# A chunked scan that feeds a feed-forward layer: two batches, not two heads, stacked in the partitions, tiles of 64 rows in TensorE, and the first feed-forward step one chunk sooner

## The chip, the cores and the metric

One core of a Trainium2 chip runs the whole program. The metric is the device time of one execution in microseconds (us), and the median of the runs is what counts. The profiled execution is one run by itself, with its own time and, beside it, the span from its first to its last instruction.

## The reference, cut to what matters

```python
# x [4, 8, 768, 32], a [4, 8, 768], B and C [4, 8, 768, 16]
for c in range(nc):
    cum = np.cumsum(log_a[chunk c])                       # per batch and head
    L = np.exp(cum[i] - cum[j]) * (i >= j)
    M = einsum('bhin,bhjn->bhij', Cc, Bc) * L
    y[chunk c] = M @ xc + einsum('bhin,bhnd->bhid', Cc, state) * np.exp(cum)
    state = exp(sum(la)) * state + sum_j (Bc[j] xc[j]) * exp(cum[-1] - cum[j])
x = y as [3072 tokens, 256]
h = x @ w_in                                              # 256 -> 2048
out = np.maximum(0.01 * h, h) @ w_out                     # 2048 -> 256
```

A state-space scan goes over 768 steps in chunks, for 4 batches and 8 heads. Its output, 3072 tokens of 256 numbers, goes through a two-layer network (FFN). The FFN's weights come as 64-bit floats, which the kernel turns into two 32-bit parts (a high part `wha` and a rest `wla`), so that each product of the FFN is a sum of three TensorE products.

## The kernel before

**Stages.** The scan takes 12 chunks (`NC`) of 64 tokens (`Q`). Within its loop run the first FFN steps, which need only the first 512 tokens, and the decoding of the first nine weight blocks (128 of the 2048 inner columns each). Behind the scan a middle phase goes through what is left of token blocks 0 and 1 (512 tokens each), and a late phase through blocks 2 to 5. The order of the instructions on each engine is the order of the code: nothing reorders it. DMAs go through SP's queue.

**One chunk c of the scan** (loop `for c in range(2, NC + 1)`), in the order in which TensorE (PE) gets its work:

- `decays`: exponents of the decay factors by one product each for two halves, into `pd` and, in the early chunks, the bank of the FFN's `h`. ScalarE (ACT) takes the exponential into `lt` (`decay_exp`).
- `scores(c)`: C times B, into the banks of `pa` and `pb` (two banks each). `bbd` is B spread by ACT (`spread_b`), so that one product gives both heads of a pair, which lie stacked in the partitions.
- `states(c-1)`: what chunk c-1 adds to the state, into a corner of `pb`.
- `passed(c+1)`: cumulated exponents, four products into another corner of `pb`. ACT takes their exponential `es` (`passed_exp`), GpSimd (POOL) multiplies it with C into `cd` (`weigh_c`).
- `weigh(c, 0)`, `weigh(c, 1)`: VectorE (DVE) multiplies the scores in `pa`, then those in `pb`, with `lt`. `keep_state(c-1)`, two operations on DVE, makes the new state `ss`.
- `ffn_in`: from chunk `FIRST` on, six products of 512 columns into `h`. ACT takes the leaky ReLU twice, DVE the rest.
- `outputs(c-1)`: a part from the state (`cd` times `ss`, the "inter" products) and a part from the chunk itself (`lt` times `x`, the "intra" products), both into `yspace`: bank pair `o01` for the first chunks, columns of `pa` later. `keep_out` copies the sum out on ACT. Two chunks (each 4 batches x 64 tokens) make one token block of 512; for chunks 0 to 3, which fill blocks 0 and 1, the copy goes to `xh`, and `low_out` on DVE takes the rest `xl`. The FFN reads these two as its high and low parts.
- `ffn_out`: six products of 512 columns into `o01`, once two steps are in the queue.

The decoding of a weight block (`dec_abs`, `dec_clamp`, `dec_shift`, `dec_sign`, `dec_low`, `dec_high`, `dec_rest`) is spread over the chunks by the table `duty`: in part -1 it stands ahead of `passed`, in part 0 ahead of `outputs`, in part 1 at the chunk's end.

**PSUM.** The scan holds seven banks besides `h`'s: `o01` (two), `pa` (two), `pb` (two) and `pd`. From chunk `FIRST - 1` on `o01` is left to the FFN's accumulation.

**The middle phase** has one step for (f, block 1) with f below `NEARLY`, and two steps for each later f; a step is six products into `h` and six into `o`.

Of the kernel before, what the change touches and what calls it, by code (L numbers as in the profile page):

```python
# [31 lines left out]
ROW = 64  # L32
PR = ROW + 6
KD = PR + 3 * GB
DIRECT = 1
SLOTS = 5
WARM = 6
FIRST = 5
# [9 lines left out]
def scan_ffn(ctx: ExitStack, tc: tile.TileContext, a_l, bcn_l, x_l, w_l, out_l):  # L48
# [142 lines left out]
    zspace = pb[:, 0, CT:CT + NB * D]  # L191
    espace = pb[:, 1, CT:]
# [22 lines left out]
    erev = cst.tile([128, NC * GB, 2], F32, name="erev")  # L215
# [8 lines left out]
    bs, cs, ts, xs, bbd, bnd, lts, es, cds, ss, tmps = ({} for _ in range(11))  # L224
# [83 lines left out]
    )  # L308
    dve.tensor_reduce(
# [76 lines left out]
    def spread_b(c):  # L386
        bbd[c] = pw.tile([128, NB, 2, Q], F32, name="bbd")
        for hp in range(2):
            act.activation(
                bbd[c][:, :, hp], bs[c].rearrange("p (b i) -> p b i", b=NB), AF.Copy,  # L390
                scale=odd[:, hp:hp + 1],
            )

    def scores(c):
        for b in range(NB):
            for g in range(NG):
                r = slice(32 * g, 32 * g + 32)
                o = b * Q
                pe.matmul(  # L399
                    (pa, pb)[g // 2][:, g % 2, o:o + Q], lhsT=bbd[c][r, b].rearrange("p h i -> p (h i)"),  # L400
                    rhs=cs[c][r, b * Q:(b + 1) * Q], start=True, stop=True,
                )

    def weigh(c, half):
        m = lts[c][:, halves[half]].rearrange("p (g b) i -> p g (b i)", g=2)
        dve.tensor_tensor(out=m, in0=(pa, pb)[half][:, :, :CT], in1=m, op=ALU.mult)

    def states(c):
        for b in range(NB):
            for g in range(NG):  # L410
                gb = g * NB + b
                pe.matmul(  # L412
                    zspace[32 * g:32 * g + 32, b * D:(b + 1) * D],
                    lhsT=bnd[c][:, gb].rearrange("p h n -> p (h n)"), rhs=xs[c][:, gb],
                    start=True, stop=True, skip_group_check=True,
                )

    def keep_state(c):
        ss[c] = p3.tile([128, NB, 2, D], F32, name="ss")
        z = zspace.rearrange("p (b d) -> p b d", b=NB)  # L420
        for hp in range(2):
            if c:
                dve.scalar_tensor_tensor(
                    out=ss[c][:, :, hp], in0=z, scalar=odd[:, hp:hp + 1], in1=tmps[c][:, :, hp],
                    op0=ALU.mult, op1=ALU.add,
                )
            else:
                dve.tensor_scalar(
                    out=ss[c][:, :, hp], in0=z, scalar1=odd[:, hp:hp + 1], scalar2=None,
                    op0=ALU.mult,  # L430
                )

    def end_decay(c):
        tmps[c] = pw.tile([128, NB, 2, D], F32, name="tmp")
        e = es[c].rearrange("p (b i) -> p b i", b=NB)[:, :, Q - 1:]
        pool.tensor_tensor(
            out=tmps[c].rearrange("p b h d -> p b (h d)"),
            in0=ss[c - 1].rearrange("p b h d -> p b (h d)"),
            in1=e.to_broadcast([128, NB, 2 * D]), op=ALU.mult,
        )  # L440

    def weigh_b(c):
        bnd[c] = pw.tile([128, GB, 2, N], F32, name="bnd")
        pool.tensor_tensor(
            out=bnd[c],
            in0=ts[c].rearrange("p (g n) -> p g n", n=N).unsqueeze(2).to_broadcast(
                [128, GB, 2, N]),
            in1=erev[:, c * GB:(c + 1) * GB].unsqueeze(3).to_broadcast([128, GB, 2, N]),
            op=ALU.mult,
        )  # L450
# [7 lines left out]
    def passed(c):  # L458
        for g in range(NG):
            pe.matmul(  # L460
                espace[32 * g:32 * g + 32],
                lhsT=dl[ROW:PR, c].rearrange("p h i -> p (h i)")[:, ::2 * Q // 32],
                rhs=dr[ROW:PR, slot(c), g * NB:(g + 1) * NB].rearrange("p g i -> p (g i)"),
                start=True, stop=True, skip_group_check=True,
            )

    def passed_exp(c):
        es[c] = p3.tile([128, CT], F32, name="es")
        act.activation(es[c], espace, AF.Exp)
# [5 lines left out]
    def outputs(c):  # L475
        mt, y = lts[c], yspace(c)
        if c:
            for b in range(NB):
                for g in range(NG):
                    r = slice(32 * g, 32 * g + 32)  # L480
                    o = 64 * (g % 2)
                    pe.matmul(  # L482
                        y[o:o + 64, g // 2, b * Q:(b + 1) * Q],
                        lhsT=ss[c - 1][r, b].rearrange("p h d -> p (h d)"),
                        rhs=cds[c][r, b * Q:(b + 1) * Q], start=(b == 0), stop=False,
                        skip_group_check=True,
                    )
        for b in range(NB):
            for h in range(NH):
                g, hp = divmod(h, 2)  # L490
                r = slice(64 * hp, 64 * hp + 64)
                o = 32 * (h % 4)
                gb = g * NB + b
                pe.matmul(  # L494
                    y[o:o + 32, h // 4, b * Q:(b + 1) * Q], lhsT=xs[c][r, gb], rhs=mt[r, gb],
                    start=(c == 0 and b == 0), stop=True, skip_group_check=True,
                )

    def keep_out(c):
        t, o = divmod(c, 2)  # L500
        cols = slice(o * CT, (o + 1) * CT)
        act.copy((xh if t < 2 else xf)[t][:, :, cols], yspace(c))

    def low_out(c):
        t, o = divmod(c, 2)
        cols = slice(o * CT, (o + 1) * CT)
        if t < 2:
            dve.tensor_tensor(
                out=xl[t][:, :, cols], in0=yspace(c), in1=xh[t][:, :, cols], op=ALU.subtract,
            )  # L510
# [19 lines left out]
    pool.memset(erev, 0.0)  # L530
# [7 lines left out]
    spread_b(0)  # L538
# [9 lines left out]
    sum_rows(1, o01[:, 0, 2 * Q:4 * Q])  # L548
# [16 lines left out]
    keep_state(0)  # L565
    passed(1)
# [10 lines left out]
    scores(1)  # L577
# [21 lines left out]
    send_rows(4, 6)  # L599
    for c in range(2, NC + 1):  # L600
# [32 lines left out]
        fetch_w(c - 2, (0,) if c > 2 else ())  # L633
# [265 lines left out]
```

## Time and profile before

| | |
|---|---|
| median of 3 runs | 322.34 us (321.31 to 322.8) |
| profiled execution | 321.72 us |
| its span, first to last instruction | 320.0 us |
| mean granted clock of TensorE | 0.993 |
| instructions | 7414 |

The profiled execution is 0.62 us below the median. Its span leaves 1.72 us of it that no instruction covers. An entry such as "32*64 32x64" is a product on a part of the array of 32 rows and 64 columns, with an operand of 32 partitions and 64 elements.

### The profile page before, as it was taken

The page shows a single profiled execution, that of the slowest core. Times are in us where ns is not written, and L with a number is a line of the kernel's source. Part 1 is how long each engine was busy: PE and PEld are TensorE (multiplying, and loading weights), DVE is VectorE, ACT ScalarE, POOL GpSimd, SP SyncE. Part 2 cuts the span into 40 slices and gives each one's busy share as a digit, 9 for nine tenths or more (in the row PEclk, how much of TensorE's full clock was granted, in tenths as well). Part 3 has the DMA queues.
Part 4 walks back from the last instruction along what each step waited for, and adds up shares of the span by engine and source line. Part 5 has one row for each costly group of instructions (what it writes and reads, how often), then busy time and mean ns, then how long its engine had stood idle before and what let it go on. Part 6 is the DMA issues. An engine that isn't in the chain of part 4 may idle for free.

```text
span 320.0 us, 7414 instructions
## 1 busy us (share of the span) xinstructions
PE 309.0 (97%) x3049; PEld 246.7 (77%) x3049; DVE 215.3 (67%) x351; ACT 189.6 (59%) x347; POOL 82.8 (26%) x103
## 2 busy tenths in 40 slices
PE   8799699999999999999999999999999999999994
PEld 3477577777788888888788888888888888888883
DVE  6558787777788999744766666775576555665551
ACT  7668667775569567643765456654475435554351
POOL 4457655662273656820000101000000000000000
PEclk9979999999999999999999999999999999999999
DMA  6759565533324100000210000000012000000003
GB/s 188 217 152 288 170 195 183 175 101 88 115 65 133 67 1 0 2 0 0 81 52 0 0 0 3 1 0 2 0 38 95 0 0 0 2 1 0 0 2 132
DMA packets 15296, 20.40 MB, mean 64 GB/s; under 512 B 3166, under 2 KB 8094, under 8 KB 15262
## 3 DMA queue, kind: packets, MB, share of 16 engines
q1 hardware_dynamic: 14910, 19.84, 19.6%
q8 instruction: 24, 0.39, 0.5%
q10 hardware_dynamic: 352, 0.09, 0.1%
q14 instruction: 10, 0.08, 0.1%
HBM read 16.62 MB, written 3.29 MB: 62 GB/s over the span
## 4 chain that ended last, share of the span: by engine, by line
PE 93%; DVE 2%; ACT 1%; DMA 1%; issue 1%; ACTq 0%
PE o L150 40%; PE h L150 37%; PE pa L399 3%; PE pa L494 3%; PE pa L482 2%; PE pd L453 1%; PE pb L412 1%; PE o L494 1%; DMA dl<-sums 1%; PE pa L246 1%; PE o L482 1%; PE pb L399 1%; PE pb L460 1%; ACT gh L804 1%; DVE gl L806 0%
## 5 line engine op out<-in xcount | busy, mean ns | idle before, releaser
L804 ACT ACTIVATE gh<-tmp 128x512 fp32r<-128x512 f32 x48 | 30.2, 629 | 49.6 <-DVE tmp L828 46.3
L806 DVE TENSOR_TENSOR gl<-tmp,gh 128x512 fp32r<-128x512 f32 x48 | 33.2, 692 | 22.2 <-ACT tmp L805 22.2
L150 PE MATMUL o<-gh,wha 128*128 128x512 f32 x108 | 42.8, 396 | 0.0
L150 PE MATMUL o<-gl,wha 128*128 128x512 f32 x108 | 42.1, 390 | 0.0
L150 PE MATMUL o<-gh,wla 128*128 128x512 f32 x108 | 42.1, 390 | 0.0
L150 PE MATMUL o<-gh,whb 128*128 128x512 f32 x84 | 32.7, 389 | 0.0
L150 PE MATMUL o<-gh,wlb 128*128 128x512 f32 x84 | 32.7, 389 | 0.0
L150 PE MATMUL o<-gl,whb 128*128 128x512 f32 x84 | 32.7, 389 | 0.0
L805 ACT ACTIVATE tmp<-tmp 128x512 f32<-128x512 f32 x48 | 30.4, 633 | 1.5
L184 DVE TENSOR_TENSOR gl<-h,gh 128x512 fp32r<-128x512 f32 x32 | 21.8, 685 | 12.3 <-ACT h L182 12.1
L181 ACT ACTIVATE gh<-h 128x512 fp32r<-128x512 f32 x32 | 19.0, 595 | 15.6 <-PE h L150 15.5
L823 DVE TENSOR_TENSOR tmp<-h,tmp 128x512 f32<-128x512 f32 x16 | 11.1, 691 | 20.8 <-PE h L150 20.8
L150 PE MATMUL h<-oph,wsh 128*128 128x512 f32 x64 | 24.9, 389 | 0.0
L150 PE MATMUL h<-oph,wsl 128*128 128x512 f32 x64 | 24.9, 389 | 0.0
L150 PE MATMUL h<-opl,wsh 128*128 128x512 f32 x64 | 24.9, 389 | 0.0
L150 PEld LDWEIGHTS o<-gh,wha 128*128 128x128 f32 x108 | 20.2, 187 | 4.6
L150 PEld LDWEIGHTS o<-gl,wha 128*128 128x128 f32 x108 | 20.3, 188 | 4.2
L150 PEld LDWEIGHTS o<-gh,wla 128*128 128x128 f32 x108 | 20.3, 188 | 4.0
L821 ACT COPY tmp<-h 128x512 f32<-128x512 f32 x16 | 9.4, 588 | 20.9 <-PE h L150 20.9
L182 ACT ACTIVATE h<-h 128x512 f32<-128x512 f32 x32 | 19.0, 595 | 0.0
L150 PEld LDWEIGHTS o<-gl,whb 128*128 128x128 f32 x84 | 15.8, 188 | 3.3
L150 PEld LDWEIGHTS o<-gh,wlb 128*128 128x128 f32 x84 | 15.8, 188 | 3.3
(154 smaller groups left out, 717.4 us busy)
## 6 DMA issues: line engine op xcount, KB each, us to landing
raw<-w_l SPq DMA_DIRECT2D x32, 256.0 KB, 3.3
xs<-x_l SPq DMA_DIRECT2D x12, 256.0 KB, 3.7
out_l<-ob SPq DMA_DIRECT2D x9, 256.0 KB, 2.3
bs<-bcn_l SPq DMA_DIRECT2D x12, 128.0 KB, 3.4
cs<-bcn_l SPq DMA_DIRECT2D x12, 128.0 KB, 3.2
ts<-bcn_l SPq DMA_DIRECT2D x12, 128.0 KB, 4.2
out_l<-wtmp SPq DMA_DIRECT2D x3, 256.0 KB, 2.5
la<-a_l SPq DMA_DIRECT2D x1, 96.0 KB
```

Of the source, the lines that this page charges most:

```text
L150: pe.matmul(space, lhsT=w, rhs=x, start=start and i == 0, stop=stop and i == 2, skip_group_check=again,)
L181: act.activation(gh, hp, AF.Prelu, alpha=0.01)
L182: act.activation(hp, hp, AF.Prelu, alpha=0.01)
L184: return lambda: dve.tensor_tensor(out=gl, in0=hp, in1=gh, op=ALU.subtract)
L399: pe.matmul((pa, pb)[g // 2][:, g % 2, o:o + Q], lhsT=bbd[c][r, b].rearrange("p h i -> p (h i)"), rhs=cs[c][r, b * Q:(b + 1) * Q], start=T ...
L482: pe.matmul(y[o:o + 64, g // 2, b * Q:(b + 1) * Q], lhsT=ss[c - 1][r, b].rearrange("p h d -> p (h d)"), rhs=cds[c][r, b * Q:(b + 1) * Q], ...
L494: pe.matmul(y[o:o + 32, h // 4, b * Q:(b + 1) * Q], lhsT=xs[c][r, gb], rhs=mt[r, gb], start=(c == 0 and b == 0), stop=True, skip_group_che ...
L804: act.activation(gh, v, AF.Prelu, alpha=0.01)
L805: act.activation(v, v, AF.Prelu, alpha=0.01)
L806: return g, lambda: dve.tensor_tensor(out=gl, in0=v, in1=gh, op=ALU.subtract)
L821: act.copy(a, A)
L823: dve.tensor_tensor(out=u2, in0=B, in1=a, op=ALU.add)
```

## The change

Two batches (`st`) instead of two heads lie stacked in the partitions; the host arrays are permuted to suit. Then B can be the stationary operand as it is (64 columns), C is spread by the parity of its head (`cm` in place of `bbd`), and `scores` and the "intra" products work on tiles of 64 rows or columns by 32, eight of which can stand in the array, in an order that names eight different ones in a row. `states` has 64 rows and 64 columns moving, `passed` is two full products of a new selector `esel` with `er`, which two new DMAs bring (`send_er`). All corners (`es`, the state, `y`) are now columns in each quarter of `pa` and `pb`: the output has half its columns in `pa` and half in `pb`, and from chunk 1 on nothing of it in `o01`. The spreading of C is shared by ACT and POOL once the FFN runs. `FIRST` goes from 5 to 4, and with it `NEARLY` from 8 to 9, the blocks decoded in the scan (`NFA`) from 9 to 10, and the table `duty` and the fetching of weights one chunk forward.

```diff
+NE = 3 * NH
-FIRST = 5
+FIRST = 4
 NEARLY = NC - FIRST + 1
 NFA = NEARLY + 1
...
-    zspace = pb[:, 0, CT:CT + NB * D]
-    espace = pb[:, 1, CT:]
+    sspace = [v.rearrange("p g (a x) -> p g a x", a=NH2)[:, :, :, :2 * Q] for v in (pa, pb)]
+    quarters = [v.rearrange("p s (a x) -> p (s a) x", a=NH2) for v in (pa, pb)]
+    espace, zspace = (v[:, :, 2 * Q:2 * Q + 2 * D] for v in quarters)
...
-    def yspace(c):
-        return o01[:, :, :CT] if c < FIRST - 1 else pa[:, :, CT:]
+    def yspace(c, m):
+        if c:
+            return quarters[m][:, :, 3 * Q:]
+        return o01.rearrange("p s (a x) -> p (s a) x", a=NH2)[:, :, m * Q:(m + 1) * Q]
...
+    def send_er(lo, hi):
+        sp.dma_start(
+            er[:, lo * 2:hi * 2],
+            sums[lo * GB:hi * GB].rearrange("(c k) p i -> (k p) c i", k=NH),
+        )
...
-    def spread_b(c):
-        bbd[c] = pw.tile([128, NB, 2, Q], F32, name="bbd")
...
+    def spread_c(c, hps=(0, 1)):
+        if c not in cms:
+            cms[c] = pw.tile([128, 2, CT], F32, name="cm")
+        for hp in hps:
+            act.activation(cms[c][:, hp], cs[c], AF.Copy, scale=odd[:, hp:hp + 1])
+
+    def spread_rest(c):
+        pool.tensor_scalar(
+            out=cms[c][:, 1], in0=cs[c], scalar1=odd[:, 1:2], scalar2=None, op0=ALU.mult,
+        )
...
     def scores(c):
         for b in range(NB):
+            bp, st = divmod(b, 2)
+            o = (st * NH2 + bp) * Q
+            cols = slice(o, o + Q)
             for g in range(NG):
                 r = slice(32 * g, 32 * g + 32)
-                o = b * Q
                 pe.matmul(
-                    (pa, pb)[g // 2][:, g % 2, o:o + Q], lhsT=bbd[c][r, b].rearrange("p h i -> p (h i)"),
-                    rhs=cs[c][r, b * Q:(b + 1) * Q], start=True, stop=True,
+                    sspace[g // 2][64 * st:64 * st + 64, g % 2, bp].rearrange(
+                        "p (h i) -> p h i", h=2),
+                    lhsT=bs[c][r, cols], rhs=cms[c][r, :, cols], start=True, stop=True,
                 )
...
     def weigh_b(c):
-        bnd[c] = pw.tile([128, GB, 2, N], F32, name="bnd")
+        bnd[c] = pw.tile([128, GB, N], F32, name="bnd")
...
     def passed(c):
-        for g in range(NG):
+        for st in range(2):
             pe.matmul(
-                espace[32 * g:32 * g + 32],
...
+                espace[:, st * NH2:(st + 1) * NH2], lhsT=esel,
+                rhs=er[:, c * 2:c * 2 + 2, st * Q:(st + 1) * Q], start=True, stop=True,
+                skip_group_check=True,
             )
...
     def outputs(c):
...
-        for b in range(NB):
-            for h in range(NH):
...
+        for m in range(2):
+            for bp in range(NH2):
+                for o in range(4):
+                    for st in range(2):
+                        r = slice(64 * st, 64 * st + 64)
+                        u = (bp * NG + 2 * m) * 2 + o
+                        pe.matmul(
+                            y[m][32 * o:32 * o + 32, st * NH2 + bp], lhsT=xs[c][r, u],
+                            rhs=mt[r, u], start=(c == 0 and m == 0 and bp == 0), stop=True,
+                            skip_group_check=True,
+                        )
...
     def keep_out(c):
         t, o = divmod(c, 2)
-        cols = slice(o * CT, (o + 1) * CT)
-        act.copy((xh if t < 2 else xf)[t][:, :, cols], yspace(c))
+        for m in range(2):
+            out = (xh if t < 2 else xf)[t][:, m, o * CT:(o + 1) * CT]
+            act.copy(out.rearrange("p (q i) -> p q i", q=NB), yspace(c, m))
...
-        o = f + 3
+        o = f + FIRST - 2
         duty[o - (f == 0), 1] += [(dec_abs, f), (dec_clamp, f)]
...
+    decode(1, 1)
     for c in range(2, NC + 1):
         f = c - FIRST
...
-            spread_b(c + 1)
+            spread_c(c + 1, (0,) if f >= 0 else (0, 1))
...
+            if f >= 0:
+                spread_rest(c + 1)
```

PE's order in a middle chunk of the loop, from the last scores to the inter products, before:

```order
L399 MATMUL pb<-cs,bbd 128x64 x2
L412 MATMUL pb<-xs,bnd 32x32 [waits DMAHW7_49]
L412 MATMUL pb<-xs,bnd 32x32 x15
L460 LDWEIGHTS dl
L460 MATMUL pb<-dr,dl 32x256
...
L150 MATMUL h_89<-xh_79,wha 128x512 [waits DVE_49]
...
L453 MATMUL pd<-dr,dl 128x512 [waits Activation_49]
L482 MATMUL pa<-cd,ss 64x64 [waits DVE_49]
L482 MATMUL pa<-cd,ss 64x64 x15
L494 MATMUL pa<-lt,xs 32x64 x32
```

And after, where L427 is `scores`, L445 `states`, L492 `passed`, L152 the FFN's products, L485 `decays`, L513 the inter and L525 the intra products:

```order
L427 MATMUL pb<-cm,bs 64x128 x2
L445 MATMUL pb<-xs,bnd 32x64 [waits DMAHW3_49]
L445 MATMUL pb<-xs,bnd 32x64 x15
L492 LDWEIGHTS esel
L492 MATMUL pa<-er,esel 128x2x64
...
L152 MATMUL h_89<-xh_79,wha 128x512 [waits DVE_49]
...
L485 MATMUL pd<-dr,dl 128x512 [waits Activation_49]
L513 MATMUL pa<-cd,ss 64x64 [waits DVE_49]
L513 MATMUL pa<-cd,ss 64x64
L513 MATMUL pb<-cd,ss 64x64 [waits DVE_49]
...
L525 MATMUL pa<-lt,xs 32x64 x16
L525 MATMUL pb<-lt,xs 32x64 x16
```

The sequence is the same; `passed` has moved from `pb` to `pa`, and the inter products wait for DVE twice: once for `weigh` on `pa` (the only wait before), and for their part in `pb` for the last operation of DVE on `pb`, the second `keep_state`.

DVE's order in such a chunk, from the decoding's shift to the FFN's rest, before:

```order
L113 TENSOR_SCALAR w_1144<-w_1144 128x512 [waits DVE_49]
L406 TENSOR_TENSOR lt<-pa,lt 128x512 [waits PE_49]
L406 TENSOR_TENSOR lt<-pb,lt 128x512 [waits Activation_49]
L423 SCALAR_TENSOR_TENSOR ss<-pb,odd,tmp 128x4x32 [waits Pool_49]
L423 SCALAR_TENSOR_TENSOR ss<-pb,odd,tmp 128x4x32
L119 SCALAR_TENSOR_TENSOR w_1144<-raw,w_1144 128x512 [waits DMAHW5_49,DMAHW3_49,DVE_49]
L125 SCALAR_TENSOR_TENSOR w_1144<-raw,w_1144 128x512 [waits DVE_49]
L184 TENSOR_TENSOR gl_61<-h_89,gh_60 128x512 [waits Activation_49]
```

And after (L435 is `weigh`, L457 `keep_state`):

```order
L115 TENSOR_SCALAR w_1031<-w_1031 128x512 [waits DVE_49]
L435 TENSOR_TENSOR lt<-pa,lt 128x2x256 [waits Activation_49]
L435 TENSOR_TENSOR lt<-pb,lt 128x2x256
L457 SCALAR_TENSOR_TENSOR ss<-pb,odd,tmp 128x4x32 [waits Pool_49]
L457 SCALAR_TENSOR_TENSOR ss<-pb,odd,tmp 128x4x32
L121 SCALAR_TENSOR_TENSOR w_1031<-raw,w_1031 128x512 [waits DMAHW3_49,DMAHW1_49,DVE_49]
L127 SCALAR_TENSOR_TENSOR w_1031<-raw,w_1031 128x512 [waits DVE_49]
L186 TENSOR_TENSOR gl_65<-h_89,gh_64 128x512 [waits Activation_49]
```

Before, the first `weigh` waits for PE's scores and only the second for `es`; after, the wait for ACT's `es` stands ahead of both, since `es` is read out of `pa`.

## Rows read from the trace of the kernel before

**Rows 1.** The page: busy time, share of the span, instructions.

```profile
PE 309.0 (97%) x3049; PEld 246.7 (77%) x3049; DVE 215.3 (67%) x351; ACT 189.6 (59%) x347; POOL 82.8 (26%) x103
```

**Rows 2.** Windows: us; busy us (count) of PE, PEld, DVE, ACT, POOL; clock; DMA.

```profile
8.24:18.48 10.24, 8.08 (x235) 5.39 (x231) 6.28 (x15) 6.81 (x15) 5.29 (x6) 1.00 0.61 172
18.48:21.89 3.41, 3.41 (x98) 2.61 (x96) 1.21 (x3) 2.21 (x5) 2.36 (x3) 0.50 0.70 171
25.30:38.95 13.65, 11.17 (x387) 8.26 (x375) 10.86 (x20) 9.29 (x20) 9.69 (x10) 1.00 0.71 220
58.47:65.44 6.97, 6.97 (x179) 5.22 (x179) 5.23 (x10) 5.04 (x11) 4.39 (x5) 1.00 0.49 155
```

**Rows 3.** Timeline of PE, one chunk: start, us, work, [idle before].

```profile
60.22 0.33 PE L399 MATMUL pa<-cs,bbd 32*128 32x64 f32 x2
...
60.38 0.28 PE L399 MATMUL pa<-cs,bbd 32*128 32x64 f32 x2
...
60.49 0.28 PE L399 MATMUL pa<-cs,bbd 32*128 32x64 f32 x2
...
61.27 0.46 PE L412 MATMUL pb<-xs,bnd 128*32 128x32 f32 x32
61.66 0.30 PE L460 MATMUL pb<-dr,dl 6*32 6x256 bf16 x4
61.89 0.50 PE L150 MATMUL h<-xh,wha 128*128 128x512 f32 x1
...
63.39 0.39 PE L453 MATMUL pd<-dr,dl 118*128 118x512 bf16 x1
63.72 0.69 PE L482 MATMUL pa<-cd,ss 32*64 32x64 f32 x32
64.34 1.10 PE L494 MATMUL pa<-lt,xs 64*32 64x64 f32 x64
65.36 0.50 PE L150 MATMUL o<-gh,wha 128*128 128x512 f32 x1
```

**Rows 4.** Timeline of DVE, the same chunk and the next chunk's first `weigh`.

```profile
61.38 0.69 DVE L406 TENSOR_TENSOR lt<-pa,lt 128x512 f32<-128x512 f32 x1
62.49 0.69 DVE L406 TENSOR_TENSOR lt<-pb,lt 128x512 f32<-128x512 f32 x1 [0.42 <-ACT es L469]
63.10 0.60 DVE L423 SCALAR_TENSOR_TENSOR ss<-pb,odd,tmp 128x128 f32<-128x128 f32 x2
63.61 0.68 DVE L119 SCALAR_TENSOR_TENSOR w<-raw,w 128x512 uint32<-128x512 uint32 x1
64.33 0.99 DVE L125 SCALAR_TENSOR_TENSOR w<-raw,w 128x512 uint32<-128x512 uint32 x1
...
68.34 0.69 DVE L406 TENSOR_TENSOR lt<-pa,lt 128x512 f32<-128x512 f32 x1
```

**Rows 5.** Timeline of ACT, the same chunk.

```profile
62.07 0.38 ACT L469 ACTIVATE es<-pb 128x256 f32<-128x256 f32 x1 [1.15 <-PE pb L460]
```

**Rows 6.** Timeline of PE, the chunks ahead of the FFN's steady state.

```profile
18.08 0.30 PE L460 MATMUL pb<-dr,dl 6*32 6x256 bf16 x4
...
19.17 1.13 PE L482 MATMUL o<-cd,ss 32*64 32x64 f32 x32
20.23 1.86 PE L494 MATMUL o<-lt,xs 64*32 64x64 f32 x64
22.02 0.33 PE L399 MATMUL pa<-cs,bbd 32*128 32x64 f32 x2
...
25.88 0.39 PE L453 MATMUL pd<-dr,dl 118*128 118x512 bf16 x1
...
33.47 0.45 PE L412 MATMUL pb<-xs,bnd 128*32 128x32 f32 x30 [1.28 <-issue]
...
45.97 0.39 PE L453 MATMUL pd<-dr,dl 118*128 118x512 bf16 x1
```

**Rows 7.** The chain that ended last, behind the scan: start, us, what.

```profile
84.96 4.08 PE h L150 x18
```

More of the change, by code (lines that the diff above doesn't have):

```diff
@@ L21 @@
 NG = NH // 2
+NH2 = NB // 2
 GB = NG * NB
@@ L214, in scan_ffn @@
     dr = cst.tile([128, SLOTS, GB, Q], BF16, name="dr")
-    erev = cst.tile([128, NC * GB, 2], F32, name="erev")
+    erev = cst.tile([128, NC * GB], F32, name="erev")
+    esel = cst.tile([NE, 128], BF16, name="esel")
+    er = cst.tile([NE, NC * 2, CT // 2], BF16, name="er")
     parts = [cst.tile([128, 3, 2 * Q], BF16, name=f"parts{i}") for i in range(2)]
@@ L222, in scan_ffn @@
     sums = dram.tile([NC * GB, 3, 2 * Q], BF16, name="sums")
-    bs, cs, ts, xs, bbd, bnd, lts, es, cds, ss, tmps = ({} for _ in range(11))
+    bs, cs, ts, xs, cms, bnd, lts, es, cds, ss, tmps = ({} for _ in range(11))
     def fetch_bc(c, which):
@@ L308, in scan_ffn @@
     )
+    pool.memset(esel, 1.0)
+    pool.affine_select(
+        out=esel, in_=esel, pattern=[[-3, NH], [0, N]], compare_op=ALU.is_ge, fill=0.0, base=0,
+        channel_multiplier=1,
+    )
+    pool.affine_select(
+        out=esel, in_=esel, pattern=[[3, NH], [0, N]], compare_op=ALU.is_ge, fill=0.0, base=2,
+        channel_multiplier=-1,
+    )
     dve.tensor_reduce(
@@ L402, in scores @@
                 )
     def weigh(c, half):
-        m = lts[c][:, halves[half]].rearrange("p (g b) i -> p g (b i)", g=2)
-        dve.tensor_tensor(out=m, in0=(pa, pb)[half][:, :, :CT], in1=m, op=ALU.mult)
+        m = lts[c].rearrange("p (a g h) i -> p a g (h i)", a=NH2, g=NG)[:, :, 2 * half:2 * half + 2]
+        dve.tensor_tensor(
+            out=m, in0=sspace[half].rearrange("p g a x -> p a g x"), in1=m, op=ALU.mult,
+        )
     def states(c):
         for b in range(NB):
+            bp, st = divmod(b, 2)
+            r = slice(64 * st, 64 * st + 64)
@@ L423, in keep_state @@
                 dve.scalar_tensor_tensor(
-                    out=ss[c][:, :, hp], in0=z, scalar=odd[:, hp:hp + 1], in1=tmps[c][:, :, hp],
-                    op0=ALU.mult, op1=ALU.add,
+                    out=ss[c][:, :, hp], in0=z[:, :, hp], scalar=odd[:, hp:hp + 1],
+                    in1=tmps[c][:, :, hp], op0=ALU.mult, op1=ALU.add,
                 )
@@ L475, in outputs @@
     def outputs(c):
-        mt, y = lts[c], yspace(c)
+        mt, y = lts[c], [yspace(c, m) for m in range(2)]
         if c:
-            for b in range(NB):
+            for q in range(NB):
                 for g in range(NG):
+                    m, o = divmod(g, 2)
                     r = slice(32 * g, 32 * g + 32)
-                    o = 64 * (g % 2)
                     pe.matmul(
-                        y[o:o + 64, g // 2, b * Q:(b + 1) * Q],
-                        lhsT=ss[c - 1][r, b].rearrange("p h d -> p (h d)"),
-                        rhs=cds[c][r, b * Q:(b + 1) * Q], start=(b == 0), stop=False,
+                        y[m][64 * o:64 * o + 64, q],
+                        lhsT=ss[c - 1][r, q].rearrange("p h d -> p (h d)"),
+                        rhs=cds[c][r, q * Q:(q + 1) * Q], start=(q % NH2 == 0), stop=False,
@@ L486, in outputs @@
                         skip_group_check=True,
                     )
-        for b in range(NB):
-            for h in range(NH):
[L490 to L497, printed above, removed]
+        for m in range(2):
+            for bp in range(NH2):
+                for o in range(4):
+                    for st in range(2):
+                        r = slice(64 * st, 64 * st + 64)
+                        u = (bp * NG + 2 * m) * 2 + o
[3 more added lines that the diff above has]
+                            skip_group_check=True,
+                        )
@@ L551, in scan_ffn @@
         decay_exp(0, h)
-    for hp in range(2):
-        p = slice(64 * hp, 64 * hp + 64)
-        act.activation(erev[p, :, hp], pcol[p], AF.Exp)
+    act.activation(erev, pcol, AF.Exp)
+    sum_rows(1, HB[0][:, :2 * Q])
     weigh_b(0)
@@ L565, in scan_ffn @@
     keep_state(0)
+    scores(1)
     passed(1)
@@ L632, in scan_ffn @@
         fetch_bc(c + 2, "b")
-        fetch_w(c - 2, (0,) if c > 2 else ())
+        fetch_w(c + 3 - FIRST, (0,))
         fetch_bc(c + 2, "c")
@@ L639, in scan_ffn @@
         low_out(c - 1)
-        fetch_w(c - 2, (1,) if c > 2 else ())
+        fetch_w(c + 3 - FIRST, (1,))
         fetch_bc(c + 2, "t")
         if c == 2:
+            send_er(8, NC)
             send_cols(8, NC, sp)
```

82 lines of the change are left out of this document (35 added, 47 removed).

## The prediction

> **What bounds the kernel now.** I read the page's first part first: TensorE (PE) is busy for 309.0 of 320.0 us, the next engine, VectorE (DVE), for 215.3 [rows 1]. As that is an average over stages, I went on to the windows. A middle chunk of the scan, 58.47 to 65.44, takes 6.97 us and PE is busy for all of it, DVE for 5.23, ScalarE (ACT) for 5.04 [rows 2]. So the scan, too, is bound by PE once the FFN runs. The chain that ended last says the same of what lies behind it: from 84.96 on it consists of FFN products alone, 4.08 us for 18, so 1.36 for six [rows 7].
>
> The timeline of PE splits the 6.97 us, from start to start [rows 3]: `scores` 61.27 - 60.22 = 1.05, `states` .39, `passed` .23, `ffn_in` 1.50, `decays` .33, inter products .62, intra products 1.02, and `ffn_out`, the same six products as `ffn_in`, 1.50; with the other `decays` of .33 this is 6.97. The reader is to see the pace in it: sets of four scores follow each other at .11 (60.38, 60.49), so the four tiles of a set run together: each pass alone takes .28, four start in .11.
>
> The other engines have little room all the same. DVE starts `weigh` on `pa` at 61.38, .11 behind the last score, ahead of `es`; it waits .42 for `es` only at `weigh` on `pb`, and is through with `keep_state` at 63.10 + .60 = 63.70 [rows 4]. The inter products start at 63.72 [rows 3]. The kernel is balanced there to .02 us, so whatever makes DVE later shows at once.
>
> **What it removes from PE.** The trace shows every product of this scan in two passes: 32 for the 16 scores, 32 for the 16 inter products, 64 for the 32 intra products [rows 3]. Scores keep their 16 products, but a tile is now 32*64, the inter products' shape, and moves 128 columns. The inter products move 64 columns and take .62 for 8 sets of four, some .06 a set behind a start of about .15 (as the first scores, 60.38 - 60.22); 128 columns would take about .11. If eight tiles run together where four did, scores need 4 sets x .11 + .15 = .60 instead of 1.05, and intra products half of 1.02 and a little for the start, .58. The trace shows no set of eight, so I keep both ends: this, and no overlap beyond four, which leaves 8 x .11 + .15 = 1.05 and 1.02. I take the full overlap, because sets of four overlap whatever the shape of their tiles (32*128, 32*64, 64*32). `states` has half the rows and twice the columns, I leave it at .37; `passed` two full products for four, .25. PE's own sum for a chunk is then .33 + .60 + .37 + .25 + 1.50 + .33 + .62 + .58 + 1.50 = 6.08, .89 less.
>
> **What it adds: a chain that PE must wait for.** The order of DVE and PE shows two new waits. `weigh` on `pa` waits for `es`, and the inter products' part in `pb` for the second `keep_state`. What is queued behind the former on DVE is both `weigh` and both `keep_state`; what waits for these is PE. From the start P of `passed`: `es` starts at +.41 (62.07 - 61.66) [rows 3, 5], `weigh` on `pa` .42 later (62.49 - 62.07) [rows 4, 5], the one on `pb` .61 after it (63.10 - 62.49), `keep_state` .61 and its .60 after that [rows 4]. That is P + 2.65; with the .02 of the balance P + 2.67. PE's cover in that time is `passed` .25, `ffn_in` 1.50 and `decays` .33 = 2.08. So PE stands still for .59 in each chunk, and the chunk takes 2.67 + .62 + .58 + 1.50 + .33 + .60 + .37 = 6.67: it saves .30 of the .89.
>
> The page "TensorEngine Tiling (Array Packing)" of the Trainium skill (PSUM Bottleneck) speaks against the change in the same way: "Tiling speeds up TensorE but not PSUM evacuation", and the copies out of PSUM may come to bound it. By the rule the .89 would be saved only as far as ACT and DVE get through PSUM; the trace's .59 of stall agrees with it.
>
> The second loop is near: from `keep_state`'s end at 63.70 to the next `weigh` at 68.34 DVE and ACT have 4.64 us of decoding and FFN work [rows 4]; with 1.82 for the three operations above it is 6.46, a lower bound for a chunk that has no `passed`.
>
> **Where the FFN doesn't cover.** Chunks 2 and 3 have no FFN. The output is in the banks of the scores now, so `scores(c)` waits for the copies and subtractions of the chunk before: two copies at about the .38 that `es` takes for 128x256 [rows 5], the second pipelined, and a last subtraction at half a `weigh`, .35 [rows 4], in all about 1.1. From `passed` to `passed` a chunk takes 2.67 + 1.20 (inter and intra) + 1.1 + .97 (scores, states) = 5.94. Before, 3.86 us lie between the products at 22.02 and 25.88 [rows 6]; at nothing before did the scores wait there. In chunk 4, the first with the FFN, DVE has sign (.72 to its next), low bits (.99), the FFN's rest (.68) and two subtractions (.35 each) behind `keep_state` [rows 4]: 3.1 from there to the next scores, 2.67 + 3.1 + .97 = 6.74.
>
> `passed(3)` starts at 18.08 before [rows 6]; I set 17.5, for one score block and one intra block less. Then `passed` of chunk 4 starts at 23.4, of 5 at 29.8 (.4 for decoding that stands ahead of the copies), of 6 at 36.5, and chunk 5 ends at 36.5 + 2.67 + 1.20 + 1.50 = 41.9. That is the FFN work that the kernel before has done at 45.97 [rows 6], one step sooner by the table. There follow five chunks of 6.67, one of 6.46, and the last without scores, 1.50 + 1.20 + 1.50 = 4.20: 85.9 to 86.0. Before, the scan's end is at 84.96 [rows 7]. **Scan +1.0, middle phase one step of 2 x 1.36 less, -2.7: -1.7.**
>
> **The clock.** Before, PE was busy for 8.08 of 10.24 us, and from 18.48 to 21.89 it was granted .50, 1.2 GHz; for 11.17 of 13.65 later and it stayed at 2.4 GHz [rows 2]. At the low level inter and intra products took 1.06 and 1.79 [rows 6] instead of .62 and 1.02 [rows 3], 1.73 times as long. With the change PE stands half idle in chunks 2 to 4 (some 2.8 busy of 5.94), with less activity than ahead of the low stretch before. I expect that stretch again, which costs 1.20 x .73 = .87 on the chain, and a second through chunk 3, (.97 + 1.20) x .73 = 1.6. Below it lies nothing more than before, above it chunk 4 as well: its scores, states, outputs (1.6) and the part of `ffn_in` that then outlasts the chain, (2.08 x 1.73 - 2.67) = .9, together 2.5.
>
> **The rest.** PE's stand-stills marked "issue", 1.28 at 33.47 for one [rows 6], will lie elsewhere; 0 to 1.3 more, I take .4. POOL gets `spread_rest` and loses half of `weigh_b`; it is busy 4.39 of 6.97 [rows 2], so this costs nothing while it has those 2.6. The two DMAs of `er` and earlier weight fetches join SP's queue; DMA share is .61 to .71 in the early chunks [rows 2], and I add nothing.
>
> **Sum.** 321.72 - 1.7 + .87 + 1.6 + .4 = 322.9 for a profiled execution. The median was .62 above it: **323.5**.
>
> **The rivals.**
> - *A, the clock is low no longer than before.* For it: a busy share of .82 kept it high [rows 2]. Against: the share falls to about a half. 323.5 - 1.6 = 321.9, no change.
> - *B, not slower: the waits are hidden.* Place: DVE's `weigh` behind `es`. If `es` comes .3 sooner (two products instead of four, and ACT idle 1.15 ahead of it [rows 5]) and the products on `pb` may start with the first `keep_state`, the stall goes: six chunks x .59 = 3.5 off, 320.0; with A's clock 318.4. It decides from a stall below .1 on. Against: each term of the chain has a row.
> - *C, the low clock lasts through chunk 4.* 326.0, more if chunk 5 has it.
> - *D, eight tiles run no faster than four.* .89 back in nine chunks, all on the chain in the early ones and past the stall in the rest: up to 8 us, 331.5; half an overlap 327.5. Against: the sets of three shapes all run together.
>
> **How the numbers follow.** Forecast .32, A .25, B .23, C .14, D .06. About 0.5%, or 1.6 us, is what a measurement here can tell from no change: faster is below 320.7, slower above 323.95. B is faster (.23); A and six tenths of the forecast's own range, 322.5 to 325, are the same (.40 with the edges); the rest of it, C and D are slower (.37). The range 318.4 to 328.0 takes in A and C, most of B and D's half, and leaves out some .13.
>
> **What would show it.** PE's timeline after: scores .60 and intra .58 in a middle chunk (else D); an idle .6 ahead of the inter products with `keep_state` as its releaser (else B); 6.0 from `passed` to `passed` in chunks 2 and 3, scores released by the copies; the clock's row at .5 from about 18 to 25 (else A or C); one middle step less. Wrong it would be if PE's stalls were filled, or if the early chunks cost more than 2 us each.

## The result, and the profile after

The change takes 325.12 us (median of 14 executions, 323.54 to 327.06), the kernel before 322.58 in the same runs: a ratio of 1.0085, 95% interval 1.0059 to 1.0111. It is slower, by more than the .5% that can be told from no change. The time lies in the predicted range, which is wide (318.4 to 328.0), and on the side that had .37, where no change had .40; the likeliest number, 323.5, was 1.6 us too low.

The page of the change, beside [rows 1]: PE is busy for about as long and stands still 3 us more, and the row of the granted clock is low in its third slice of 8 us and partly in its fourth.

```profile
span 321.8 us, 7390 instructions
PE 307.7 (96%) x3026; PEld 240.2 (75%) x3027; DVE 217.2 (67%) x354; ACT 187.7 (58%) x351; POOL 90.0 (28%) x115
PEclk9957999999999999999999999999999999999999
```

The timeline of PE in a middle chunk of the change, beside [rows 3]:

```profile
58.15 0.33 PE L427 MATMUL pa<-cm,bs 32*64 32x128 f32 x2
...
58.77 0.46 PE L445 MATMUL pb<-xs,bnd 64*32 64x64 f32 x32
59.16 0.28 PE L492 MATMUL pa<-er,esel 24*128 24x128 bf16 x2
59.37 0.50 PE L152 MATMUL h<-xh,wha 128*128 128x512 f32 x1
...
60.86 0.39 PE L485 MATMUL pd<-dr,dl 118*128 118x512 bf16 x1
61.18 0.33 PE L513 MATMUL pa<-cd,ss 32*64 32x64 f32 x4
61.81 0.27 PE L513 MATMUL pb<-cd,ss 32*64 32x64 f32 x2 [0.30 <-DVE ss L457]
...
62.42 0.45 PE L525 MATMUL pa<-lt,xs 64*32 64x64 f32 x32
62.69 0.59 PE L525 MATMUL pb<-lt,xs 64*32 64x64 f32 x32
63.21 0.50 PE L152 MATMUL o<-gh,wha 128*128 128x512 f32 x1
```

The next scores start at 65.03, so a chunk takes 6.88 (6.97 before). Scores take .62 instead of 1.05. Then the inter products start in `pa` at once, stop behind the first two products (x4: each product runs in two passes), and go on at 61.81 when `keep_state` is through; from 61.18 to 62.42 they take 1.24 instead of .62, .30 of it without any product. The intra products take .27 for the half in `pa` and .52 for the half in `pb`. DVE and ACT show the chain:

```profile
59.95 0.69 DVE L435 TENSOR_TENSOR lt<-pa,lt 128x512 f32<-128x512 f32 x1
60.56 0.68 DVE L435 TENSOR_TENSOR lt<-pb,lt 128x512 f32<-128x512 f32 x1
61.16 0.60 DVE L457 SCALAR_TENSOR_TENSOR ss<-pb,odd,tmp 128x128 f32<-128x128 f32 x2
```

```profile
59.53 0.39 ACT L500 ACTIVATE es<-pa 128x256 f32<-128x256 f32 x1 [0.68 <-PE pa L492]
```

`weigh` on `pa` starts .42 behind `es` (before, ahead of it), and `keep_state` ends at 61.76, 2.60 behind `passed`. But `es` is not alone in holding it. DVE is busy up to 59.87 with the clamp (L110) and the shift (L115) of a weight block, so `weigh` stands only .08 behind its own engine's work. The clamp takes longer than before; the first row is of the kernel before (L108), and the last is the POOL operation that runs beside it in the change:

```profile
60.09 0.71 DVE L108 TENSOR_SCALAR w<-w 128x512 f32<-128x512 f32 x1 [1.13 <-ACT w L105]
58.30 1.10 DVE L110 TENSOR_SCALAR w<-w 128x512 f32<-128x512 f32 x1 [1.20 <-ACT w L107]
59.44 0.43 DVE L115 TENSOR_SCALAR w<-w 128x512 uint32<-128x512 uint32 x1
57.84 1.28 POOL L136 TENSOR_TENSOR wla<-w,wha 128x512 fp32r<-128x512 f32 x1
```

This POOL operation lies beside the clamp for .82 in the change and for .43 before (59.24 to 60.52); a clamp with no POOL operation beside it takes .43 in both kernels (39.86 before, 30.46 in the change).

The middle chunks are not where the time went. The starts of `passed` tell it: of chunks 3 to 6 they are at 17.47, 24.63, 31.54 and 38.52, before at 18.08, 23.46, 27.64 and 33.85 (18.08 in [rows 6]; the others are the starts of the same product in the same view). The change is .6 us ahead, then 1.2, 3.9 and 4.7 behind, and stays there: the products behind the scan that end the chain begin 4.6 us later (89.53 against 84.96 in [rows 7]), and the middle phase then gives one step of 2.72 back. The rows from `passed(4)` to the next scores show both causes, first by the timeline of PE:

```profile
24.63 0.28 PE L492 MATMUL pa<-er,esel 24*128 24x128 bf16 x2
24.84 0.39 PE L485 MATMUL pd<-dr,dl 118*128 118x512 bf16 x1
26.16 0.33 PE L513 MATMUL pa<-cd,ss 32*64 32x64 f32 x4 [0.93 <-DVE lt L435]
27.27 0.32 PE L513 MATMUL pb<-cd,ss 32*64 32x64 f32 x2 [0.79 <-DVE ss L457]
...
28.28 0.68 PE L525 MATMUL pa<-lt,xs 64*32 64x64 f32 x32
28.70 0.76 PE L525 MATMUL pb<-lt,xs 64*32 64x64 f32 x32
29.39 0.61 PE L485 MATMUL pd<-dr,dl 118*128 118x512 bf16 x1
29.95 0.69 PE L427 MATMUL pa<-cm,bs 32*64 32x128 f32 x4
30.38 0.48 PE L427 MATMUL pb<-cm,bs 32*64 32x128 f32 x2
```

PE stands still for 1.7 us ahead of and within the inter products. The scores in `pa` start right behind DVE's subtraction of the output there, those in `pb` behind the second; PE has `decays` to do up to about 30.0, so that the wait costs it some .4 here, an estimate from these rows (30.38 less 30.0):

```profile
29.47 0.42 DVE L545 TENSOR_TENSOR xl<-pa,xh 128x256 fp32r<-128x256 f32 x1 [1.65 <-ACT xh L535]
29.90 0.42 DVE L545 TENSOR_TENSOR xl<-pb,xh 128x256 fp32r<-128x256 f32 x1
```

Ahead of chunk 5 the same wait is PE's longest stand-still within the loop. Its row names POOL's `bnd`, but the subtraction from `pa` ends at the same 37.14, and of the two it is the subtraction that the scores need, as they write the bank that it reads:

```profile
37.24 0.43 PE L427 MATMUL pa<-cm,bs 32*64 32x128 f32 x4 [1.26 <-POOL bnd L478]
36.71 0.43 DVE L545 TENSOR_TENSOR xl<-pa,xh 128x256 fp32r<-128x256 f32 x1 [0.35 <-ACT xh L535]
```

Second, by the windows (columns as in [rows 2]), the clock:

```profile
16.95:23.85 6.90, 5.96 (x159) 3.65 (x159) 4.41 (x9) 4.21 (x10) 2.49 (x3) 0.51 0.60 169
23.85:27.27 3.42, 1.71 (x67) 0.91 (x51) 1.85 (x5) 1.66 (x4) 0.73 (x1) 0.98 0.83 266
27.27:30.65 3.38, 3.38 (x106) 2.50 (x113) 1.58 (x4) 2.14 (x5) 2.75 (x3) 0.51 0.84 239
```

10.3 us are at the low level, 1.2 GHz, where the profile before has 3.4 [rows 2]; ahead of the second such stretch PE was busy for 1.71 of 3.42 us.

### The profile page after: what moved, and what is told of

The parts are those of the page before. It is cut to its first block, busy times and chain, and to the rows that moved or that the text cites. A ratio compares the mean times of both kernels' runs of the same rounds, so it can differ in the third digit from the quotient of the medians.

```text
span 321.8 us, 7390 instructions
## 1 busy us (share of the span) xinstructions
PE 307.7 (96%) x3026; PEld 240.2 (75%) x3027; DVE 217.2 (67%) x354; ACT 187.7 (58%) x351; POOL 90.0 (28%) x115
## 4 chain that ended last, share of the span: by engine, by line
PE 78%; DVE 9%; DMA 4%; issue 3%; ACT 3%; POOL 2%; SPq 0%; ACTq 0%; POOLq 0%; DVEq 0%
PE o L152 38%; PE h L152 33%; DVE lt L435 3%; DMA raw<-w_l 3%; DVE ss L457 2%; POOL cm L416 1%; PE pb L513 1%; PE pa L427 1%; PE pa L525 1%; PE pa L254 1%; ACT es L500 1%; PE pb L525 1%; PE pb L445 1%; DMA cs<-bcn_l 1%; PE pb L427 1%
## 5 line engine op out<-in xcount | busy, mean ns | idle before, releaser
L152 PE MATMUL o<-gh,wha 128*128 128x512 f32 x120 | 47.6, 397 | 0.0
L152 PE MATMUL o<-gl,wha 128*128 128x512 f32 x120 | 46.8, 390 | 0.0
L152 PE MATMUL o<-gh,wla 128*128 128x512 f32 x120 | 46.7, 389 | 0.0
L152 PE MATMUL o<-gh,whb 128*128 128x512 f32 x72 | 28.0, 389 | 0.0
L152 PE MATMUL o<-gh,wlb 128*128 128x512 f32 x72 | 28.0, 389 | 0.0
L152 PE MATMUL o<-gl,whb 128*128 128x512 f32 x72 | 28.0, 389 | 0.0
L152 PEld LDWEIGHTS o<-gh,wha 128*128 128x128 f32 x120 | 22.5, 188 | 5.1
L152 PEld LDWEIGHTS o<-gl,wha 128*128 128x128 f32 x120 | 22.5, 188 | 4.8
L152 PEld LDWEIGHTS o<-gh,wla 128*128 128x128 f32 x120 | 22.5, 188 | 4.4
L860 DVE TENSOR_TENSOR tmp<-h,tmp 128x512 f32<-128x512 f32 x16 | 11.1, 691 | 20.8 <-PE h L152 20.8
L152 PE MATMUL h<-oph,wsh 128*128 128x512 f32 x64 | 24.9, 389 | 0.0
L152 PE MATMUL h<-oph,wsl 128*128 128x512 f32 x64 | 24.9, 389 | 0.0
L152 PE MATMUL h<-opl,wsh 128*128 128x512 f32 x64 | 24.9, 389 | 0.0
L110 DVE TENSOR_SCALAR w<-w 128x512 f32<-128x512 f32 x16 | 12.1, 758 | 10.7 <-ACT w L107 10.4
L863 DVE TENSOR_TENSOR tmp<-h,tmp 128x512 f32<-128x512 f32 x16 | 11.1, 692 | 8.7 <-PE h L152 8.6
```

The lines of the kernel that those rows point to most:

```text
L110: dve.tensor_scalar(out=w32(f), in0=w32(f), scalar1=MAG_MIN, scalar2=MAG_MAX, op0=ALU.max, op1=ALU.min,)
L152: pe.matmul(space, lhsT=w, rhs=x, start=start and i == 0, stop=stop and i == 2, skip_group_check=again,)
L860: dve.tensor_tensor(out=u2, in0=B, in1=a, op=ALU.add)
L863: dve.tensor_tensor(out=u3, in0=E, in1=u2, op=ALU.add)
```

## The experiments

The theory T was that the loss lies in the layout: the stall of the inter products, the early chunks whose scores wait for the copies, and the clock that falls. The rivals: R1, the sooner FFN step costs; R2, the clock is nearly all of it; R3, DVE and ACT are the bound behind the stall. Times are ratios to the kernel before, from the same runs on the same chip, with their 95% intervals. The change was not run again beside its variants: "less than the change" compares two such ratios. The mean granted clock of each execution is known too, and stands below as "clocks" where it bears on a reading.

**The sooner FFN step taken back (e1), and made alone (b1).**

```diff
-FIRST = 4
+FIRST = 5
```

> The change with its first FFN step put back to chunk 5 (nine blocks decoded in the scan), the new layout kept. Theory T (the loss lies in the layout: the stall of the inter products in each middle chunk, the early chunks whose scores wait for the copies of the output, and the low clock that follows): chunk 4 loses an FFN step and with it about 1.0, chunk 5 has no ffn_out and loses about 1.3, the middle phase gets a step of 2.7 back: 325.5, within 1 us of the change (325.1). Rival R1 (the sooner FFN step, with its decoding and weight fetches, is what costs): back to the time before, 322.6, or below.

Measured: 1.0110 (1.0060 to 1.0159). The layout alone is as slow as the whole change, as T has it; R1 falls as the only cause. The clocks of its six executions are .953 to .969, those of the change .963 to .983. The profile, its slowest execution, shows the clock at the low level for 30.8 us:

```profile
14.60:45.40 30.80, 26.68 (x592) 16.18 (x595) 16.14 (x33) 15.65 (x34) 12.03 (x17) 0.50 0.61 185
```

The kernel before, with the step:

```diff
-FIRST = 5
+FIRST = 4
...
-        o = f + 3
+        o = f + FIRST - 2
...
+    decode(1, 1)
     for c in range(2, NC + 1):
...
-        fetch_w(c - 2, (0,) if c > 2 else ())
+        fetch_w(c + 3 - FIRST, (0,))
```

> The kernel before with the first FFN step, the table of the decoding and the weight fetches one chunk forward (ten blocks decoded in the scan), and its old layout. Rival R1 (the sooner FFN step is what costs): 1% slower than before, or as much as the change. Theory T (the layout costs): the scan gets a step of ffn_in and one of ffn_out, up to 3.0, the middle phase loses one of 2.7: a ratio of 1.000 within .004.

Measured: 1.0042 (1.0008 to 1.0076), at the edge of what T allowed for (1.004), and about half of what the change costs. But `yspace` hangs on `FIRST`: the output of chunk 3 moves from `o01` into `pa`, and in PE's timeline the scores of chunk 5 wait for its subtraction:

```profile
34.77 0.32 PE L399 MATMUL pa<-cs,bbd 32*128 32x64 f32 x2 [2.17 <-DVE xl L508]
```

So the output of chunk 3 was put back into `o01` (b2):

```diff
-        return o01[:, :, :CT] if c < FIRST - 1 else pa[:, :, CT:]
+        return o01[:, :, :CT] if c < FIRST else pa[:, :, CT:]
```

> The kernel before with the sooner FFN step, as b1, but the output of chunk 3 kept in o01, so that scores(5) doesn't wait for its subtraction from the banks of the scores (2.17 in b1's profile). Theory T (output in the banks of the scores is what costs, in either layout): 1.5 to 2.5 us less than b1, ratio to before .996 to 1.000. Rival R1 (the sooner FFN step itself costs): as b1, 1.004 or more.

Measured: 1.0015 (.9979 to 1.0052). The wait of 2.17 is gone from its profile. That is .3% below b1, less than the 1.5 to 2.5 us that T expected, and its interval overlaps with b1's. It lies between the two expectations and can't be told from either's edge; that the FFN step by itself costs is not shown, nor that it costs nothing.

**The corners of es and state exchanged (e2).**

```diff
-    espace, zspace = (v[:, :, 2 * Q:2 * Q + 2 * D] for v in quarters)
+    zspace, espace = (v[:, :, 2 * Q:2 * Q + 2 * D] for v in quarters)
```

> The change with the corners of es and of the state exchanged: the state's in pa, es in pb, so that the first weigh waits for PE alone and the inter products' part in pb no longer waits for keep_state. Theory T: the idle time ahead of the inter products goes in all chunks (.30 and the slow first set, together about .6 of 6.88), a middle chunk takes 6.3 to 6.5, chunks 2 to 4 lose about .5 each: 4 us less, 321. Rival R1 (the FFN step) or R2 (the clock alone): no more than 1 us less, 324. Rival R3 (DVE and ACT are the bound behind the stall): a middle chunk stays above 6.7 and the idle time moves to the scores or to ffn_in: 324.5.

Measured: .9998 (.9962 to 1.0033), .9% less than the change, though its clocks are lower (median .970, the change's .980). A middle chunk takes 6.70, not 6.3 to 6.5. The chain through `es` is gone, and R3 is right about what comes next:

```profile
58.59 1.10 DVE L110 TENSOR_SCALAR w<-w 128x512 f32<-128x512 f32 x1 [1.20 <-ACT w L107]
59.72 0.43 DVE L115 TENSOR_SCALAR w<-w 128x512 uint32<-128x512 uint32 x1
60.06 0.68 DVE L435 TENSOR_TENSOR lt<-pa,lt 128x512 f32<-128x512 f32 x1
```

```profile
61.92 0.27 PE L513 MATMUL pa<-cd,ss 32*64 32x64 f32 x2 [0.37 <-DVE ss L457]
```

The scores end near 59.1, yet `weigh` starts at 60.06: DVE has the clamp and shift of a weight block ahead of it, which wait for ACT's abs, which stands behind the copies of the output. PE still waits .37 for `keep_state`. So the places of `es` and the state cost a middle chunk .18 (6.88 to 6.70); behind it DVE's own work, with the clamp of 1.10, held `weigh` back almost as long.

**Half of the early output in o01 (e3).**

```diff
-        if c:
+        if c and (m == 0 or c >= FIRST):
             return quarters[m][:, :, 3 * Q:]
```

> The change with the second half of the output of chunks 1 to 3 in the bank pair o01 instead of pb, so that the scores in pb don't wait for its copy and subtraction. Theory T: the scores in chunks 3 to 5 still wait for the copy and subtraction of pa, which come first, so each saves about .4, together 1.2, and more if the clock stays high: 322.5 to 324. Rival (the early chunks are bound by the chain through weigh and keep_state alone, not by the copies): no change, 325.

Measured: .9984 (.9949 to 1.0019), 1.0% less than the change. From `passed(3)` to `passed(5)` it takes 12.15 us instead of 14.07, and the second low stretch of the clock is missing from its profile: .52 from 17 to 24, .99 from 24 to 31. Over its twelve executions the clocks are no higher than the change's (median .973 and .980), so the gain is not the clock's.

```profile
17.00:24.00 7.00, 6.38 (x200) 3.78 (x196) 4.25 (x9) 4.04 (x9) 2.49 (x3) 0.52 0.58 158
24.00:31.00 7.00, 4.81 (x171) 3.33 (x170) 5.16 (x11) 4.68 (x11) 4.22 (x5) 0.99 0.90 256
```

**Idle products against the low clock (e4).**

```diff
+        if c < FIRST:
+            keep_warm(4, o01[:, 0])
         outputs(c - 1)
```

> The change with four products of 512 columns on idle data into o01 ahead of the inter products in chunks 2 to 4, which compute nothing that is used; they fill most of the time in which PE waits for weigh. Rival R2 (most of the loss is the low clock): the granted clock stays at 1.0 from 17 to 31 us, and the time falls by 3 us or more to 322. Theory T: the clock is a part: 1.5 to 2.5 us less, 323, the chain through es, weigh and keep_state being left. If the products delay the inter products, no gain, 325.

Measured: .9969 (.9941 to .9998), 1.2% or 3.7 us less than the change, for 8 products whose results nobody reads (the condition holds in chunks 2 and 3 alone, not in 4 as the expectation has it). In its profile, its slowest execution, the clock is low in two stretches, and high in between, where it falls in the change:

```profile
14.60:21.60 7.00, 6.34 (x85) 2.65 (x89) 4.28 (x10) 5.58 (x11) 3.26 (x6) 0.51 0.62 190
38.40:42.00 3.60, 3.60 (x39) 2.27 (x37) 3.38 (x7) 1.95 (x5) 2.14 (x3) 0.53 0.49 155
```

That is as long as in the profile of the change (10.6 and 10.3 us), its fastest execution. All executions together tell it better: the clocks are .983 to .994 here and .963 to .983 in the change, and where they are the same, .983 to .984, so are the times: 323.7 to 323.9 here, 323.5 and 324.1 in the change. So the gain is the clock's, and R2 has its 3 us, though not by holding the clock throughout.

**er first (f1).**

```diff
+    send_er(1, 3)
     send_rows(1, 4)
-    send_er(1, 8)
+    send_er(3, 8)
```

> The change with the DMA that brings er split and its part for chunks 1 and 2 sent ahead of the two DMAs of send_rows(1, 4), so that passed(1) doesn't wait for it. If the late er is a cost of its own (passed(1) waits 1.2 to 1.7 in four of five profiles, and the low clock begins behind it): passed(1) starts .5 to 1.0 sooner, 1 to 2.5 us less than the change, a ratio to before of 1.000 to 1.005. Rival (the wait is hidden, since decays(1) waits for the rows of send_rows anyway, which now come later): no change, 1.0085.

Measured: 1.0092 (1.0058 to 1.0126). `passed(1)` starts at 12.59, without a wait, instead of 12.90 to 13.35 in the profiles of the change and of e1 to e4, and nothing comes of it, as the rival has it: a miss for the idea that this DMA costs.

**The remedies together (f2), and the decoding moved (f3).**

```diff
     scores(1)
+    keep_warm(2, pd)
     passed(1)
...
+    keep_warm(3, o01[:, 0])
     for c in range(2, NC + 1):
```

These stand beside the edits of e2, e3, e4 and f1.

> The four remedies together on the change: corners of es and state exchanged, the second half of y of chunks 1 to 3 in o01, er first, and idle products ahead of passed(1), ahead of chunk 2 and in chunks 2 to 4. Theory T (stall, early chunks and clock are separate sums): a middle chunk 6.70 as in the run with the exchanged corners, the early chunks as in the run with o01 or better, clock at 1.0 throughout: 3 to 5 us less than before, 318.5, ratio .985 to .991. If the idle products or the order of DMAs cost as much as they give: .995.

Measured: .9908 (.9874 to .9943), at the upper edge of T's range. The clocks are .989 to .999; in its profile, its slowest execution, the level is low from 22.7 to 29.5 us, so 1.0 throughout did not hold there.

```diff
-        duty[o - (f == 0), 1] += [(dec_abs, f), (dec_clamp, f)]
...
+            duty[o, 1].append((dec_abs, f))
+            duty[o + 1, 0] += [(g, f) for g in (dec_clamp, dec_shift, dec_sign, dec_low)]
+            duty[o + 1, 1].insert(0, (dec_high, f))
```

> The same, and from the third decoded block on the clamp and shift stand behind keep_state instead of ahead of weigh on DVE, and the copy of the high part behind keep_out on ACT. Theory T with the loop of DVE and ACT as the next bound (clamp and shift lie between abs and weigh: the middle chunk of 6.70 contains 1.45 of them): a middle chunk of 6.25 to 6.4, 2 to 3 us less than without, ratio .978 to .984. Rival (PE is the bound at 6.7): the same as without.

Measured: .9962 (.9931 to .9993), a miss: 1.6 us slower than without by the medians (321.98 and 320.38, taken together). A middle chunk takes 6.52 on average (four from `passed` at 43.16 to 69.24), 6.60 in f2; most of the wait has only moved, to the exponential of the decays, which now stands on ACT behind the copy of the high part:

```profile
63.03 0.69 DVE L435 TENSOR_TENSOR lt<-pa,lt 128x512 f32<-128x512 f32 x1 [1.18 <-ACT lt L405]
```

and the last two chunks are 1.7 us longer than in f2 (outputs to outputs 6.97 and 5.60, against 6.13 and 4.70). Whether these two chunks make the whole 1.6 is not shown.

**The wait for the first weights (g1, g3).** In f2's profile the first abs waits for its weights on ACT, with `es` of chunk 3 queued behind it; the inter products of chunk 2 stand still for 2.91:

```profile
18.50 0.66 ACT L107 ACTIVATE w<-raw 128x512 f32<-128x512 f32 x1 [1.67 <-DMA raw<-w_l]
19.06 0.37 ACT L500 ACTIVATE es<-pb 128x256 f32<-128x256 f32 x1
```

```profile
21.47 0.27 PE L513 MATMUL pa<-cd,ss 32*64 32x64 f32 x2 [2.91 <-DVE ss L457]
```

```diff
-    decode(1, 1)
...
+        if c == 2:
+            decode(1, 1)
         decode(c, 0)
```

> The four remedies (f2_best), and the first block's abs and clamp moved from ahead of the loop to behind keep_state of chunk 2, since in f2's profile the abs waits 1.67 for its weights on ACT with es of chunk 3 queued behind it, and the inter products of chunk 2 stand still for 2.91. If that wait is on the chain: 1 to 2 us less than f2_best, ratio .984 to .988. Rival (the weights are late and something else in chunk 2 waits as long): .991.

Measured: .9889 (.9861 to .9918), the fastest version, 1.1% below the kernel before and 1.9% below the change. The stall of 2.91 is .57 in its profile, but the ratio can't be told from f2's. The move alone:

> The change with that move alone. If the wait for the first weights costs in the change as well (0 to 1.7 in its runs' profiles, and with it the low clock): a ratio of 1.003 to 1.006 instead of 1.0085. Rival (the weights have landed in most executions, as in the change's own profile, where the abs starts without a wait): 1.0085.

Measured: 1.0054 (1.0020 to 1.0089), within the first expectation, but the interval takes in the rival's 1.0085 as well: inconclusive.

**Another order of the intra products (g4).**

```diff
-        for m in range(2):
-            for bp in range(NH2):
-                for o in range(4):
+        for bp in range(NH2):
+            for i in range(4):
+                for m in range(2):
                     for st in range(2):
+                        o = (i + 2 * m) % 4
```

> The change with the intra products in another order: pa and pb in turn, with eight different tiles in every eight, instead of all of pa and then all of pb. In the change the first 32 passes start in .24 and the 32 into pb take .41. If the change of banks breaks the overlap of eight: intra .6 instead of .79, .2 less in each of nine chunks, a ratio of 1.003. Rival (it is the tiles, or the operands of the second half): .79 as before, 1.0085.

Measured: 1.0119 (1.0094 to 1.0145), with clocks of .963 to .969, the lower end of the change's, and .79 again, from 58.68 to 59.47:

```profile
58.68 0.25 PE L526 MATMUL pa<-lt,xs 64*32 64x64 f32 x2
...
58.91 0.34 PE L526 MATMUL pa<-lt,xs 64*32 64x64 f32 x5
...
59.30 0.23 PE L526 MATMUL pb<-lt,xs 64*32 64x64 f32 x2
59.47 0.50 PE L152 MATMUL o<-gh,wha 128*128 128x512 f32 x1
```

Up to 58.91 some 32 passes start, in .23 (.27 in the change); the second half takes the rest, though both banks are in both halves. It is not the change of banks; what it is stays open.

## Why the prediction was right, and where it was not

**Eight tiles run together: right for the scores, mis-sized for the intra products.** Scores .62 for .60. The term "intra products half of 1.02 and a little for the start, .58" measured .79. Its first half keeps the pace of eight at once, its second half does not. Rival D falls: the scores take .62 in every middle chunk, the full overlap.

**The chain that PE must wait for: right in its times, but `es` is not its only cause.** Predicted `keep_state` through at `passed` + 2.65 and PE idle for .59; measured 2.60, the products in `pb` at + 2.65, and .30 idle after two products of `pa` in .33. The chunk was to take 6.67 and takes 6.88; the .21 are the intra products'. Rival B, the waits hidden, is refuted by the row at 61.81. The second loop was near, as the prediction says: its lower bound was 6.46, and e2 shows 6.70 without the chain, which so costs .18. The .24 between may come from a term that was put at nothing, POOL's additional work: the clamp takes .39 longer than before, and POOL works beside it for .39 longer. That the one makes the other is argued from these rows; no run tries it alone.

**Where the FFN doesn't cover: right.** `passed` of chunks 3 to 6 was to start, with the clock's terms, at 17.5, 24.3, 32.3 and 39.0; it starts at 17.47, 24.63, 31.54 and 38.52. e3, which frees half of the scores from the copies, gains 1.0%. b1 shows the same wait in the old layout (2.17); that it costs time there is not shown clear of the noise (b2).

**The sum: near, in part by errors that cancel.** With the clock's terms and the .4 the scan's end was to lie at 88.8, and lies at 89.53. From `passed(4)` to `passed(5)` it was to take 8.0 and took 6.91. The .4 for stand-stills marked "issue" came to nothing: behind 10 us the scan of the change has none in its profile, where the kernel before has three, 2.48 in all. Against this stand 1.05 us in five middle chunks and .6 behind them.

**The clock: right in kind, too small for the median.** A second stretch was expected, through chunk 3, and it lies there; the first is 6.9 us long instead of 3.4. But the profiled execution is the fastest of the 14, at 323.54, against 322.9 predicted for it. Its mean clock is .983, which no other exceeds; the slower ones go down to .963, and e1, e2 and g3 show profiles with 20 to 31 us at the low level. The step that failed is "the median was .62 above it": the change's is 1.58 above, as the low level lasts longer in most of its executions (rival C's side, without a fixed place). That the clock costs is shown by e4, 1.2% for idle products.

The clocks of all executions say more. In the runs beside the experiments the 72 executions of the kernel before that enter the ratios have clocks of .981 to 1.000, median .993. Twelve of them at .981 to .984 take 325.2 us (median), seven of the change at .981 to .983 take 324.4. At the same clock the change is not slower, so its 2.5 us go with its lower clock, and R2 holds for the difference from the kernel before. The waits of the layout cost as well, since e2 and e3 gain at clocks no higher than the change's. That these waits are what lets the clock fall fits T; e4, which fills some of them, is the one run that bears on it. Why one execution has 10 us at the low level and another 20 was not tried.

**DMAs: "I add nothing" holds for er** (f1), and is open for the first weights (g3).

**One step less in the middle phase**: right, the scan's end is 4.6 later and the span 1.8 longer, which differ by 2.8, about the predicted 2.7.

## What to carry to other kernels

When products get shorter by sharing the array, look at which bank each reader and writer now shares: here PE's products got .66 a chunk shorter and the chunk .09; the rest went into waits. .18 of it came only from where `es` and the state lie, and one exchanged line took .9% of the time back. Look at the other engines' work beside it too: a term for POOL that was put at nothing stood beside a DVE operation that took 1.10 us instead of .71. A stage whose engine has nothing to do while it waits may pay twice, once for the wait and once for the clock behind it; a few idle products there were worth 1.2%. And after a chain is cut, the next one is near: cutting the first brought 6.88 to 6.70, though the products of a chunk, with no idle time between, add up to 6.26.

## What was not expected of the hardware

64 passes of 64*32 tiles don't run at one pace: in the change the first 32 take .27 us, and the next 32 take .52 up to the start of the FFN's product; in g4, with both banks in both halves, .23 and .56. The same operation on DVE takes .43, .71 or 1.10 us, as POOL works beside it for 0, .43 or .82 us. The low level of the clock lasted from 0 us (f3) to 30.8 us (e1) in profiles of kernels that differ by a few lines in the first 40 us.
